# Sparse attention with two mixer layers: local scores as one 64x64 matmul per head

## The chip, the core and the metric

One core of a Trainium2 chip runs the whole program: TensorE (PE) multiplies, VectorE (DVE), ScalarE (ACT) and GpSimd (POOL) work on what it leaves, SyncE (SP) starts most of the DMAs. The metric is the time of one execution on the device in microseconds. The kernel before took 983.25 us (median of three runs, 981.56 to 983.28).

## The reference

Attention over four batches, eight heads, 576 tokens and 64 channels a head. Heads 0 to 3 are local (a query sees itself and the 31 tokens before it), heads 4 to 7 strided. Two mixer layers follow, each with a 512 to 2048 to 512 feed-forward part (FFN), which is most of the arithmetic.

```python
scores = 1 / np.sqrt(D) * np.matmul(q, k.transpose(0, 1, 3, 2))
rel = pos[:, None] - pos[None, :]
mask_local = (rel >= 0) & (rel < 32)
mask_strided = (rel >= 0) & (pos[None, :] % 32 == pos[:, None] % 32)
...
attn = softmax(np.where(masks, scores, -1e9))     # heads 0..3 local, 4..7 strided
x = np.matmul(attn, v)                            # then (B, S, 512)
...
u = x + (x.T @ U @ V).T                           # mixer 1: over tokens
y = u + np.maximum(u @ w_ch1, 0.0) @ w_ch2        # FFN of layer 1
...
u = y + np.real(np.fft.fft2(y))                   # mixer 2
out = u + np.maximum(norm(u) @ w21, 0.0) @ w22    # FFN of layer 2
```

## The kernel before, in words

**Stages.** Attention of batch 0, its token mix and the first weights come first (the startup). Then a main stream of FFN chunks runs on PE: lines 797 to 799 are the first FFN matmuls, lines 823 to 825 the second, in f16 pairs. Between them a fixed table (`TICKS`, then `RATES`) gives steps to two side streams: one makes FFN weights (raw 64-bit words are loaded, made into f32 by ACT and DVE, lines 133 to 137, then split), the other runs the attention of batches 1 to 3, the layout of FFN inputs and the Fourier part. The tile scheduler puts the instructions of all streams into one order for each engine by its own priorities and estimates; within an engine they then run in that order.

**Local attention.** A pair j of local heads (0 and 1, or 2 and 3) stands in SBUF with one head's 64 channels on partitions 0 to 63 and the other's on 64 to 127: k as 640 columns (tokens), q as columns of queries. A unit, `local_unit(b, j, u)`, scores four windows of 64 queries against 96 keys each (one window of u = 1 has 128). Line 386 writes the masks of all four windows into a PSUM bank (bf16 identity times mask), line 390 adds one f32 matmul a window on top. So that one matmul gives both heads, the queries were laid out with zeros: 128 columns a window, the first 64 with head 0's queries on the upper 64 partitions and zeros below, the others the reverse. Row 0 to 63 of the result is then head 0, row 64 to 127 head 1. Each batch has four units, so 16 such matmuls, 64 in all. Softmax follows (lines 357 to 365: DVE takes the maximum, ACT the exponential), then transposes on PE (line 398), an ACT copy (line 400), the product with v (line 406: weights of 64 columns, on the left or right half of the array) and the division.

**The rest.** Line 456 scores the 32 tokens left over of each half, with weights of 64 columns and all 128 partitions, left and right half of the array in turn, both into one bank. Line 472 takes their product with v on tiles of 64 rows by 32 columns: the upper rows (j = 0) into one bank, the lower (j = 1) into another. Line 422 is the strided scores.

**Loads.** `qk_load` (lines 301 to 314) brings k and q of a pair with two DMAs from SP's queue. Two local pairs stand early in the startup's list of loads (`LOADS`); each later pair takes a buffer that comes free, and batch 1's wait (line 296) until the first token mix is done.

Of the kernel before, what the change touches and what calls it, by code (L numbers as in the profile page):

```python
# [25 lines left out]
SG = 11  # L26
# [24 lines left out]


class Lane:
    """A stream of steps; a step that yields a name waits until that name is in flags."""

    def __init__(self, gen, flags):
        self.gen, self.flags = gen, flags
# [12 lines left out]
def fused_kernel(ctx: ExitStack, tc: tile.TileContext, ql, kl, vl, vr, qs, ks, vs, uraw, vraw,  # L70
                 w11, w12, w21, w22, cb, cf, ft, out):
    nc = tc.nc
    V, A, T, G, S = nc.vector, nc.scalar, nc.tensor, nc.gpsimd, nc.sync
# [15 lines left out]
    def bank():  # L89
        if wnow[0]:  # L90
            nbk[0] += 1
            z = BSEQ[nbk[0] % len(BSEQ)]
            if z:
                return (pf1, pf2)[z - 1].tile([128, 512], F32, tag=f"f{z}", name="bk")
        return pb.tile([128, 512], F32, tag="b", name="bk")
# [16 lines left out]
    flags = set()  # L112
# [133 lines left out]
    def p_buf():  # L246
        if wnow[0]:
            return early_buf("gh", 416)
        return atp.tile([128, 416], F32, tag="P", bufs=PB, name="P")

    def pt_buf():
        if wnow[0]:
            return early_buf("gl", 512)
        return atp.tile([128, 512], F32, tag="PT", bufs=PTB, name="PT")
# [39 lines left out]
    def gate(b, ap):  # L294
        if b == 1:
            A.activation(out=ap, in_=late[0], func=AF.Copy)
# [4 lines left out]
    def qk_load():  # L301
        b, x, j = QK[len(qk)]
        if len(qk) == 3:
            z = ub[3].rearrange("p a n -> p (a n)")
            q, k = z[:, 0:108 * SG], z[:, 108 * SG:108 * SG + 640]
        else:
            q = cst.tile([128, 108 * SG], F32, tag="q", bufs=3, name="q")
            k = cst.tile([128, 640], F32, tag="k", bufs=3, name="k")
            gate(b, q[0:1, 0:1])
            gate(b, k[0:1, 0:1])  # L310
        nq, nk = (1152, 640) if x == "l" else (108 * SG, 54 * SG)
        S.dma_start(out=k[:, 0:nk], in_=(kl if x == "l" else ks)[b, j])
        S.dma_start(out=q[:, 0:nq], in_=(ql if x == "l" else qs)[b, j])
        qk.append((q, k))

    def qk_upto(n):
        while len(qk) < min(n, len(QK)):
            qk_load()
# [23 lines left out]
    def first_loads():  # L342
        for x in LOADS:
            if x == "w":
                pre.append(wload(w11, len(pre), S))
            elif x == "m":
                mix_raw()
            elif x[0] in "ls":
                qk_load()
            else:  # L350
                loaded[x] = VT[x[0]](0, int(x[1:] or 0))

    def softmax_rows(P, Sb, r, groups):
        mx = atp.tile([128, 8], F32, tag="mx", bufs=3, name="mx")
        c = 0
        for o, n, w in groups:
            V.tensor_reduce(out=mx[r, c:c + n], in_=Sb[r, o:o + n * w].rearrange("p (n w) -> p n w", n=n),
                            axis=AX.X, op=ALU.max)
            c += n
        V.tensor_scalar(out=mx[r, 0:c], in0=mx[r, 0:c], scalar1=-0.125, scalar2=None, op0=ALU.mult)  # L360
        c = 0
        for o, n, w in groups:
            for i in range(n):
                a = o + i * w
                A.activation(out=P[r, a:a + w], in_=Sb[r, a:a + w], func=AF.Exp,  # L365
                             scale=0.125, bias=mx[r, c:c + 1])
                c += 1
# [5 lines left out]
    def norm_out(O, dst, r, n):  # L373
        Ov = O[r, 0:130 * n].rearrange("p (n h w) -> p n h w", h=2, w=65)
        rc = atp.tile([128, 3, 2, 1], F32, tag="rc", bufs=3, name="rc")
        recip(rc[r, 0:n], Ov[:, :, :, 64:65])
        V.tensor_tensor(out=dst.rearrange("p n (h w) -> p n h w", h=2), in0=Ov[:, :, :, 0:64],
                        in1=rc[r, 0:n].to_broadcast([r.stop - r.start, n, 2, 64]), op=ALU.mult)
# [4 lines left out]
    def local_unit(b, j, u, q, k, v):  # L383
        Sb = bank()
        n = LCOLS[u]
        T.matmul(Sb[:, 0:n], lhsT=idb, rhs=mL[u], start=True, stop=True)
        for g, x, o, w in LU[u]:
            w0 = LWIN[g, x][0]
            i = 128 * (2 * g + x)
            T.matmul(Sb[:, o:o + w], lhsT=q[:, i:i + 128], rhs=k[:, w0:w0 + w], start=False, stop=True,  # L390
                     skip_group_check=True)
        P = p_buf()
        softmax_rows(P, Sb, FULL, [(0, 3, 96), (288, 1, 128)] if u else [(0, 4, 96)])
        yield
        Tb = bank()
        m = 128 if u else 96
        for i, (g, x, o, w) in enumerate(LU[u]):
            T.transpose(Tb[0:m, 128 * i:128 * i + 128], P[:, o:o + m], ident)
        PT = pt_buf()
        A.activation(out=PT[0:m], in_=Tb[0:m], func=AF.Copy)  # L400
        yield
        O = bank()
        for i, (g, x, o, w) in enumerate(LU[u]):
            for h in range(2):
                c = 65 * (2 * (g % 2) + h)
                T.matmul(O[64 * x:64 * x + 64, c:c + 65],
                         lhsT=PT[0:w, 128 * i + 64 * h:128 * i + 64 * h + 64],
                         rhs=v[0:w, h, 2 * g + x, :], start=True, stop=True, skip_group_check=True)
        norm_out(O, ub[b][:, 2 * u:2 * u + 2, 128 * j:128 * j + 128], FULL, 2)
        yield  # L410
# [39 lines left out]
    def rest_unit(b, qks, v):  # L450
        p0 = 32 * b
        Sb = bank()
        T.matmul(Sb[:, 0:128], lhsT=idb, rhs=mX, start=True, stop=True)
        for j, (q, k) in enumerate(qks):
            for f in range(2):
                T.matmul(Sb[64 * f:64 * f + 64, 64 * j:64 * j + 64], lhsT=q[:, 1024 + 64 * f:1088 + 64 * f],
                         rhs=k[:, RWIN[f]:RWIN[f] + 64], start=False, stop=True, skip_group_check=True)
        P = p_buf()
        softmax_rows(P, Sb, FULL, [(0, 2, 64)])
        yield  # L460
        Tb = bank()
        T.transpose(Tb[:, 0:128], P[:, 0:128], ident)
        PT = pt_buf()
        A.activation(out=PT[:, 0:128], in_=Tb[:, 0:128], func=AF.Copy)
        yield
        r = slice(p0, p0 + 32)
        for j in range(2):
            O = bank()
            for f in range(2):
                for h in range(2):  # L470
                    c = 65 * (2 * f + h)
                    T.matmul(O[r, c:c + 65], lhsT=PT[64 * j:64 * j + 64, 64 * f + 32 * h:64 * f + 32 * h + 32],
                             rhs=v[64 * j:64 * j + 64, f, h, :], start=True, stop=True,
                             skip_group_check=True, tile_position=(64 * j, p0))
            norm_out(O, ur[r, :, 128 * j:128 * j + 128], r, 2)
        yield
# [461 lines left out]
    q = [0]  # L938
# [20 lines left out]
def _layout(np, q, k, v, mU, mV, w11, w12, w21, w22):  # L959
    import ml_dtypes  # L960
    pos, tiles, groups = _tok()
    f32 = np.float32
    B = q.shape[0]
# [3 lines left out]
    def put(dst, src, toks):  # L967
        i = [c for c, t in enumerate(toks) if t >= 0]
        dst[..., i] = src[:, [toks[c] for c in i]].transpose(0, 2, 1)

    def putv(dst, src, toks):
        i = [c for c, t in enumerate(toks) if t >= 0]
        dst[:, i, 0:64] = src[:, [toks[c] for c in i]]
        dst[:, i, 64] = 1.0

    ql = np.zeros((B, 2, 128, 1152), f32)
    kl = np.zeros((B, 2, 128, 640), f32)
    vl = np.zeros((B, 2, 128, 2, 8, 65), f32)
    vr = np.zeros((B, 128, 2, 2, 65), f32)
# [3 lines left out]
    for j in range(2):  # L983
        for hh in range(2):
            r = slice(64 * hh, 64 * hh + 64)
            h = 2 * j + hh
            put(kl[:, j, r], k[:, h], kext)
            for i in range(8):
                o = 128 * i + 64 * hh
                put(ql[:, j, r, o:o + 64], q[:, h], wins[i])  # L990
                w0, w = LWIN[i // 2, i % 2]
                putv(vl[:, j, :, hh, i], v[:, h], kext[w0:w0 + w])
            for f in range(2):
                o = 1024 + 64 * f + 32 * hh
                put(ql[:, j, r, o:o + 32], q[:, h], tiles[4 + f])
                putv(vr[:, 64 * j:64 * j + 64, f, hh], v[:, h], kext[RWIN[f]:RWIN[f] + 64])
            h += 4
            for i, toks in enumerate(groups):
                put(qs[:, j, r, 108 * i + 54 * hh:108 * i + 54 * hh + 54], q[:, h], toks)
                put(ks[:, j, r, 54 * i:54 * i + 54], k[:, h], toks)  # L1000
                t, e = divmod(i + (i > 0), 2)
                putv(vs[:, j, 64 * e:64 * e + 64, t, hh], v[:, h], toks)
    neg = -1e30
    mL = []
    for u in range(2):
        m = np.full((128, LCOLS[u]), neg, f32)
        for g, x, o, w in LU[u]:
            w0 = LWIN[g, x][0]
# [102 lines left out]
```

## Time and profile before

| what | value |
|---|---|
| median of three runs | 983.25 us (981.56 to 983.28) |
| span of the profiled execution | 979.2 us |
| what lies around the span, against the median | 4.05 us |
| PE busy | 935.3 us, 96% |
| weight loads of PE (PEld) busy | 522.8 us, 53% |
| DVE, ACT, POOL busy | 531.8, 360.4, 60.3 us |
| DMA | 76.53 MB, 78 GB/s mean |

The span is from the first instruction to the last; the time of an execution holds a little more. The profile gives no device time of its own for this execution, so what lies around its span is taken against the median. PE is the engine that is nearly always at work. Its matmuls are pipelined: a row's own duration is from its start to the modelled end of its last result, so how long one keeps the next from starting is read from the starts, not from the durations. f32 matmuls appear as two weight loads and two matmuls each.

### The profile page before, as it was taken

How to read it: one execution, taken by the hardware profiler on the slowest of the kernel's cores; microseconds unless marked ns; L12 is line 12 of the kernel's file. 1: busy time of each engine (PE TensorE's matmuls, PEld its weight loads, DVE VectorE, ACT ScalarE, POOL GpSimd, SP SyncE). 2: the span in 40 equal slices, each digit the busy share in tenths (PEclk: the TensorE clock that was granted, in tenths of full speed). 3: DMA queues.
4: the chain of work that ended last, by engine and by line, in shares of the span. 5: the costliest groups of instructions: out<-in, count | busy, mean ns of one | idle time of the engine just before them, and what ended most of it. 6: DMA issues, size and time to landing. Idle time of an engine off the chain costs nothing. (4 is left out here: it accounts for less than half of the span.)

```text
span 979.2 us, 13687 instructions
## 1 busy us (share of the span) xinstructions
PE 935.3 (96%) x5264; PEld 522.8 (53%) x5264; DVE 531.8 (54%) x1346; ACT 360.4 (37%) x885; POOL 60.3 (6%) x88
## 2 busy tenths in 40 slices
PE   4958999999999999999999989999999999999998
PEld 3746765556545564466445545544554444444465
DVE  4578798833342336853979998884235212122222
ACT  4667677624131334531546554231122101111011
POOL 0010111000000000100110400001001000100000
PEclk9558999999999999999999999999999999999999
DMA  9357666332201103602332610011002100300200
GB/s 301 131 175 236 217 217 212 95 115 94 64 16 28 39 3 116 172 1 44 108 107 88 151 44 1 1 33 55 1 1 43 44 1 6 80 1 1 46 20 22
DMA packets 60464, 76.53 MB, mean 78 GB/s; under 512 B 38064, under 2 KB 43440, under 8 KB 60400
## 3 DMA queue, kind: packets, MB, share of 16 engines
q1 hardware_dynamic: 51376, 42.53, 15.2%
q0 software_dynamic: 9024, 33.14, 10.6%
q8 instruction: 41, 0.67, 0.3%
q14 instruction: 23, 0.19, 0.1%
HBM read 60.18 MB, written 7.08 MB: 69 GB/s over the span
## 5 line engine op out<-in xcount | busy, mean ns | idle before, releaser
L797 PE MATMUL f<-ut,wslot 128*128 128x512 f16 (+1 forms) x672 | 236.1, 351 | 5.9 <-DVE gl L804 5.2
L798 PE MATMUL f<-ut,wslot 128*128 128x512 f16 (+1 forms) x672 | 235.8, 351 | 1.1 <-DMA ut<-lo 1.1
L799 PE MATMUL f<-ut,wslot 128*128 128x512 f16 (+1 forms) x672 | 235.6, 351 | 0.0
L823 PE MATMUL f<-wslot,gh 128*128 128x512 f16 x576 | 218.1, 379 | 0.9 <-DVE ub L831 0.5
L824 PE MATMUL f<-wslot,gh 128*128 128x512 f16 x576 | 218.1, 379 | 0.1
L825 PE MATMUL f<-wslot,gl 128*128 128x512 f16 x576 | 218.1, 379 | 0.0
L803 ACT ACTIVATE gh<-f 128x512 f16<-128x512 f32 (+1 forms) x168 | 89.4, 533 | 305.6 <-PE f L799 305.2
L804 DVE SCALAR_TENSOR_TENSOR gl<-f,gh 128x512 f16<-128x512 f32 (+1 forms) x168 | 102.8, 612 | 146.3 <-ACT gh L803 145.6
L831 DVE SCALAR_TENSOR_TENSOR ub<-f,ivt,ub 128x512 f32<-128x512 f32 x64 | 47.9, 748 | 130.1 <-PE f L825 129.8
L798 PEld LDWEIGHTS <-wslot 128*128 128x128 f16 x672 | 66.3, 99 | 64.3 <-issue 10.6
L797 PEld LDWEIGHTS <-wslot 128*128 128x128 f16 x672 | 66.4, 99 | 59.9 <-issue 4.9
L799 PEld LDWEIGHTS <-wslot 128*128 128x128 f16 x672 | 66.2, 98 | 58.9 <-issue 1.1
L825 PEld LDWEIGHTS <-gl 128*128 128x128 f16 x576 | 56.5, 98 | 66.9 <-issue 0.3
L823 PEld LDWEIGHTS <-gh 128*128 128x128 f16 x576 | 57.0, 99 | 63.8 <-issue 1.2
L824 PEld LDWEIGHTS <-gh 128*128 128x128 f16 x576 | 56.7, 98 | 62.7 <-issue 1.5
L153 ACT ACTIVATE wslot<-wslot,wsc 128x512 f16<-128x512 f32 x64 | 46.0, 718 | 43.1 <-DVE wslot L156 20.2
L133 ACT ACTIVATE wslot<-raw 128x512 f32<-128x512 f32 x64 | 42.9, 676 | 27.9 <-DMA raw<-in_w 26.5
L160 POOL DMA_DIRECT2D raw<-in_w x61 | 33.3, 546 | 319.1 <-DVE wslot L137 62.7
L156 DVE SCALAR_TENSOR_TENSOR wslot<-wslot,wsc 128x512 f16<-128x512 f32 x64 | 48.6, 760 | 7.6 <-ACT wslot L153 7.3
L197 ACT ACTIVATE wslot<-wslot 128x512 bf16<-128x512 f32 x64 | 40.3, 630 | 20.3 <-DVE wslot L137 15.9
L365 ACT ACTIVATE P<-bk,mx 108x64 f32<-108x64 f32 (+2 forms) x126 | 31.2, 328 | 39.2 <-DVE mx L360 35.9
L137 DVE SCALAR_TENSOR_TENSOR wslot<-raw,wslot 128x512 int32<-128x512 int32 x64 | 44.4, 697 | 0.1
(222 smaller groups left out, 953.3 us busy)
## 6 DMA issues: line engine op xcount, KB each, us to landing
raw<-in_w POOLq DMA_DIRECT2D x61, 512.0 KB, 4.0
q<-in_ql SPq DMA_DIRECT2D x8, 576.0 KB
q<-in_qs SPq DMA_DIRECT2D x7, 594.0 KB
out<-ub SPq DMA_DIRECT2D x16, 256.0 KB
vl<-in_vl SPq DMA_DIRECT2D x8, 390.0 KB
vs<-in_vs SPq DMA_DIRECT2D x8, 390.0 KB
k<-in_kl SPq DMA_DIRECT2D x8, 320.0 KB
scr<-xs SPq DMA_DIRECT2D x8, 270.0 KB
```

The source lines that it names most:

```text
L137: V.scalar_tensor_tensor(out=d, in0=hi, scalar=-0x80000000, in1=d, op0=ALU.bitwise_and, op1=ALU.bitwise_or)
L153: A.activation(out=dst, in_=src, func=AF.Copy, scale=s)
L156: V.scalar_tensor_tensor(out=dst, in0=src, scalar=s, in1=hi, op0=ALU.mult, op1=ALU.subtract)
L797: T.matmul(ps[:, 0:n], lhsT=wh, rhs=uh[:, k, cols], start=(k == 0), stop=False)
L798: T.matmul(ps[:, 0:n], lhsT=wh, rhs=ul[:, k, cols], start=False, stop=False)
L799: T.matmul(ps[:, 0:n], lhsT=wl, rhs=uh[:, k, cols], start=False, stop=(k == 3))
L803: A.activation(out=gh[:, i, cols], in_=ps[:, 0:n], func=AF.Relu)
L804: V.scalar_tensor_tensor(out=gl[:, i, cols], in0=ps[:, 0:n], scalar=0.0, in1=gh[:, i, cols], op0=ALU.max, op1=ALU.subtract)
L823: T.matmul(ps, lhsT=ga, rhs=w[:, 0, :], start=(i == 0), stop=False)
L824: T.matmul(ps, lhsT=ga, rhs=w[:, 1, :], start=False, stop=False)
L825: T.matmul(ps, lhsT=gb, rhs=w[:, 0, :], start=False, stop=(i == HW - 1))
L831: V.scalar_tensor_tensor(out=utile(t), in0=ps, scalar=iv, in1=utile(t), op0=ALU.mult, op1=ALU.add)
```

## The change

The queries of a local pair are laid out without the zeros: 64 columns a window, head 0 on the upper partitions, head 1 on the lower. The array q of a pair goes from 1152 to 640 columns (the 128 of the rest tokens keep their form and move from column 1024 to 512). Line 390's matmul of 128 by 128 becomes two of 64 by 64, one for each head: the upper left quarter of the array for head 0, the lower right for head 1. Both write the same bank, on partitions 0 to 63 and 64 to 127. Masks, softmax and all that follows are the same. An emptied comment line keeps the numbers up to 390; the new matmul is line 391, and all lines behind it are one higher than before.

```diff
@@ qk_load
-        nq, nk = (1152, 640) if x == "l" else (108 * SG, 54 * SG)
+        nq, nk = (640, 640) if x == "l" else (108 * SG, 54 * SG)
@@ local_unit
             w0 = LWIN[g, x][0]
-            i = 128 * (2 * g + x)
-            T.matmul(Sb[:, o:o + w], lhsT=q[:, i:i + 128], rhs=k[:, w0:w0 + w], start=False, stop=True,
-                     skip_group_check=True)
+            i = 64 * (2 * g + x)
+            for r in (slice(0, 64), slice(64, 128)):
+                T.matmul(Sb[r, o:o + w], lhsT=q[r, i:i + 64], rhs=k[r, w0:w0 + w], start=False, stop=True,
+                         skip_group_check=True)
@@ rest_unit
-                T.matmul(Sb[64 * f:64 * f + 64, 64 * j:64 * j + 64], lhsT=q[:, 1024 + 64 * f:1088 + 64 * f],
+                T.matmul(Sb[64 * f:64 * f + 64, 64 * j:64 * j + 64], lhsT=q[:, 512 + 64 * f:576 + 64 * f],
@@ _layout
-    ql = np.zeros((B, 2, 128, 1152), f32)
+    ql = np.zeros((B, 2, 128, 640), f32)
...
-                o = 128 * i + 64 * hh
+                o = 64 * i
                 put(ql[:, j, r, o:o + 64], q[:, h], wins[i])
...
-                o = 1024 + 64 * f + 32 * hh
+                o = 512 + 64 * f + 32 * hh
```

The scheduler sees twice the matmuls and sets some orders anew. On PE, at batch 1's second local unit, before (line 398 are transposes of the unit ahead, line 386 the mask, line 390 the scores; `bk` is a PSUM bank):

```order
L398 MATMUL bk<-ident,P 96x128
L386 LDWEIGHTS cbt
L386 MATMUL bk<-cbt 128x384
L398 MATMUL bk<-ident,P 96x128
L390 MATMUL bk<-k,q 128x96
L398 MATMUL bk<-ident,P 96x128 x2
L390 MATMUL bk<-k,q 128x96 x3
```

The same place on PE with the change (line 399 are the transposes, line 391 the scores):

```order
L399 MATMUL bk<-ident,P 96x128
L386 LDWEIGHTS cbt
L386 MATMUL bk<-cbt 128x384
L399 MATMUL bk<-ident,P 96x128
L391 MATMUL bk<-k,q 64x96
L399 MATMUL bk<-ident,P 96x128 x2
L391 MATMUL bk<-k,q 64x96 x7
```

The first score matmul still stands alone between transposes, but it is now one head's quarter; its partner stands behind the transposes with the other six. Six of the twelve units of batches 1 to 3 are parted so, a seventh as five and three; five stand in one piece.

On PE, at batch 1's scores of the rest tokens, before (line 453 is their mask, line 456 the scores, lines 797 to 799 the FFN):

```order
L398 MATMUL bk<-ident,P 128x128
L453 LDWEIGHTS cbt
L453 MATMUL bk<-cbt 128x128
L456 MATMUL bk<-k,q 64x64 x4
L797 LDWEIGHTS wslot
L797 MATMUL f_1206<-ut_614,wslot 128x256
L398 MATMUL bk<-ident,P 128x128
```

The same place on PE with the change (line 454 the mask, line 457 the scores):

```order
L399 MATMUL bk<-ident,P 128x128
L454 LDWEIGHTS cbt
L454 MATMUL bk<-cbt 128x128
L457 MATMUL bk<-k,q 64x64
L399 MATMUL bk<-ident,P 128x128
L457 MATMUL bk<-k,q 64x64 x2
L399 MATMUL bk<-ident,P 128x128 x2
L457 MATMUL bk<-k,q 64x64
```

The four matmuls on halves of the array stood together and now stand as one, two and one, with full-array transposes between. In batches 2 and 3 they stay together.

## Rows read from the trace of the kernel before

**Rows 1.** The page's totals: engine, busy us, share of the span, instructions.
```profile
PE 935.3 (96%) x5264; PEld 522.8 (53%) x5264; DVE 531.8 (54%) x1346; ACT 360.4 (37%) x885; POOL 60.3 (6%) x88
```

**Rows 2.** Busy time by stretch of the span; columns in the first row.
```profile
core 0: us, PE busy (x) PEld busy (x) DVE busy (x) ACT busy (x) POOL busy (x), PEclk, DMA share, GB/s
0.00:20.00 20.00, 8.52 (x52) 6.76 (x53) 7.05 (x21) 7.34 (x20) 1.42 (x6) 1.00 0.91 277
...
84.00:120.00 36.00, 32.03 (x330) 26.53 (x329) 28.49 (x87) 25.60 (x76) 3.70 (x7) 1.00 0.65 210
120.00:176.00 56.00, 53.40 (x305) 30.57 (x303) 50.44 (x102) 42.77 (x102) 7.92 (x15) 1.00 0.62 201
176.00:200.00 24.00, 23.71 (x172) 14.08 (x171) 19.86 (x57) 15.59 (x38) 0.00 (x0) 1.00 0.29 66
200.00:340.00 140.00, 140.00 (x848) 76.60 (x848) 50.31 (x116) 42.07 (x108) 0.00 (x0) 1.00 0.21 62
```

**Rows 3.** PE's waits, 82 to 200 us: waiting for, us, times, longest.
```profile
PE bk L398 <- ACT P L365: 2.7, 3, 1.3
PE bk L522 <- ACT x L518: 1.3, 2, 0.8
```

**Rows 4.** Line 390's instructions: count, ns min/median/max, first and last start, form.
```profile
L390 PEld LDWEIGHTS bk<-k,q x128: 187/192/337, 9.6 to 325.1; 128*128 128x128 f32 x128
L390 PE MATMUL bk<-k,q x128: 246/275/497, 9.6 to 325.2; 128*128 128x96 f32 x112, 128*128 128x128 f32 x16
```

**Rows 5.** Timeline at batch 2's first unit: start, us together, what, count.
```profile
177.56 0.33 PE L386 MATMUL bk<-cbt 128*128 128x384 bf16 x1
...
177.72 1.03 PE L390 MATMUL bk<-k,q 128*128 128x96 f32 x8
...
178.59 0.38 PE L797 MATMUL f<-ut,wslot 128*128 128x512 f16 x1
```

**Rows 6.** Timeline of PE at 95: two passes between transposes.
```profile
95.10 0.36 PE L390 MATMUL bk<-k,q 128*128 128x96 f32 x2
```

**Rows 7.** Timeline of PE in the startup; in brackets its idle time before.
```profile
9.62 1.99 PE L390 MATMUL bk<-k,q 128*128 128x96 f32 x8 [4.81 <-DMA q<-in_ql]
...
18.67 2.02 PE L390 MATMUL bk<-k,q 128*128 128x96 f32 x16 [1.07 <-DMA q<-in_ql]
```

**Rows 8.** Line 456's instructions (weights of 64 columns).
```profile
L456 PEld LDWEIGHTS bk<-k,q x32: 132/138/231, 27.1 to 332.1; 128*64 128x64 f32 x32
L456 PE MATMUL bk<-k,q x32: 222/222/369, 27.1 to 332.1; 128*64 128x64 f32 x32
```

**Rows 9.** Line 472 (tiles of 64 rows): first four, all sixteen, durations.
```profile
112.62 0.41 PE L472 MATMUL bk<-vr,PT 64*32 64x65 f32 x4
...
112.62 0.90 PE L472 MATMUL bk<-vr,PT 64*32 64x65 f32 x16
...
L472 PE MATMUL bk<-vr,PT x48: 214/217/241, 112.6 to 340.0; 64*32 64x65 f32 x48
```

**Rows 10.** Timeline at batch 1's rest scores, line 456, between full-array matmuls.
```profile
108.50 0.22 PE L453 MATMUL bk<-cbt 128*128 128x128 bf16 x1
...
108.65 0.31 PEld L456 LDWEIGHTS bk<-k,q 128*64 128x64 f32 x8 [0.16 <-issue]
108.65 0.45 PE L456 MATMUL bk<-k,q 128*64 128x64 f32 x8
...
109.03 0.28 PE L797 MATMUL f<-ut,wslot 128*128 128x256 f16 x1
```

**Rows 11.** Timeline of ACT in batch 1's attention.
```profile
93.45 0.66 ACT L133 ACTIVATE wslot<-raw 128x512 f32<-128x512 f32 x1 [1.42 <-DMA raw<-in_w]
```

**Rows 12.** The page's DMA issues: what, queue, count, size.
```profile
q<-in_ql SPq DMA_DIRECT2D x8, 576.0 KB
```

**Rows 13.** Timeline of PE ahead of the first FFN matmul.
```profile
74.96 1.22 PE L592 MATMUL bk<-idh,gh 128*128 128x128 f16 x8 [8.27 <-ACT gh L153]
```

## The prediction

> **What bounds the kernel now.** I read the page's totals first: TensorE (PE) is busy for 96% of the span [rows 1]. A mean over stages says little, so next the busy time by stretch [rows 2]: from 200 to 340 us PE is busy for all of the 140 us, from 176 to 200 for 23.71 of 24. There every microsecond that PE saves or loses is in the time. From 84 to 120 and from 120 to 176 it is busy for 32.03 of 36 and 53.40 of 56, so it waits for 6.6 us in all, mostly for results of ACT [rows 3]. Then the line that is changed [rows 4]: 128 weight loads and 128 matmuls, so each of the 64 local score matmuls is two passes. Four units of four windows belong to each batch. Batch 0 runs before the first FFN (its first pass at 9.62), batch 1 around 95, batch 2 from 177, batch 3 to 325 [rows 4 to 7]. So batches 2 and 3 lie where PE never waits, batch 1 where it waits a little, batch 0 in the start, which waits for loads.
>
> **The unit before.** At the full level of the clock (2.4 GHz, granted 1.00 [rows 2]) a unit's eight passes start at 177.72 and the next line starts at 178.59: 0.87 us, or 0.109 a pass [rows 5]. What sets this step? The pair at 95.10 lasts 0.36 together, so the second starts 0.36 - 0.275 = 0.085 behind the first [rows 4, 6]: with its weights already in place, 96 columns need 0.085. The steady 0.109 is then the load. A load of 128 columns takes 192 ns and one of 64 columns 138 [rows 4, 8]: 54 ns for 64 columns, so 0.108 for 128. The mask matmul stands 0.16 ahead of the first pass, which is its own stream of 384 columns: going over from it costs nothing [rows 5].
>
> **The unit after.** A quarter loads 64 columns (0.054) but streams the same 96 or 128 columns of keys: the halved contraction shortens nothing. So each pass takes 0.085, the stream is now the limit, and a 128-column window takes a third more. Do the two heads run side by side? In the rest unit's output line two row tiles at the same columns do: the first four passes, all on the upper rows, start (0.41 - 0.217)/3 = 0.064 apart, all sixteen (0.90 - 0.217)/15 = 0.046 apart [rows 9]. Column halves do too: the eight passes of line 456 last 0.45 together, less 0.22 for the last is 0.23 for seven steps, 0.033 each and so less than one load of 0.054 [rows 8, 10]. So I take the quarters as parallel: 8 x 0.085 = 0.68 a unit, a gain of 0.19.
>
> Those two rows leave one thing open: the row tiles of [rows 9] write to two PSUM banks, the column halves of [rows 10] to one bank but over all rows; no row shows two row tiles on one bank, which is what the change does. The Trainium skill speaks against it here: TensorEngine Tiling (Array Packing), section Restrictions and Gotchas, says that different row tiles cannot access the same bank simultaneously. By that rule the unit's passes would take turns, 0.68 more a unit; by the rows they don't. No trace here shows it, and it is a rival below.
>
> **What a visit to a small tile costs.** Line 453 (full array) starts at 108.50, line 456 on halves at 108.65, the next full-array matmul at 109.03 [rows 10]: 0.53. Off this go line 453's own 128 columns (0.05, a third of the 0.16 of [rows 5]) and four loads a half (4 x 0.054 = 0.22): about 0.25 remains for emptying the array twice and for the first load, which nothing covers (the loader stands idle for 0.16 there). A unit in one piece is then 0.68 + 0.25 = 0.93 against 0.87; with the 128-column window 0.1 more than before. Mean over the two: +0.075, for 12 units +0.9.
>
> The order adds more. In batches 1 to 3 the scheduler makes 19 visits of these 12 units: six units are parted 1 + 7 by full-array transposes and one 5 + 3. Before, a parting cost nothing. Now each adds 0.25, and 0.17 in which only one of the two quarters works (two passes): 0.42 x 7 = 2.9. Four are in batch 1, two in batch 2, one in batch 3. Batch 1's rest scores also go from one visit to three: 2 x 0.25 and one more pair, 0.6. By batch: 1: 0.3 + 1.7 + 0.6 = 2.6. 2: 0.3 + 0.8 = 1.15. 3: 0.3 + 0.4 = 0.7.
>
> Batches 2 and 3 are on the path: +1.9 (bounds 0.5, if a parting's extra visit were free, and 2.5). Batch 1: 2.6 against 6.6 of waits in the 92 us behind 84. Where PE waits for a weight or a softmax that hangs on DMA (ACT stands 1.42 for a raw weight at 93.45 [rows 11]), it may come later without harm; where ACT waits for PE's scores, the delay goes round. Bounds 0 and 2.6; I take 1.0, a little under half, since the waits are more than twice the delay. DVE and ACT get no other work, and their reads of the scores are the same.
>
> **The loads.** Each q load shrinks from 576 KB [rows 12] to 320 KB. 262,000 bytes at the 277 GB/s of the first 20 us [rows 2] are 0.95 us. PE stands 4.81 for the first q and 1.07 for the second [rows 7], whose SP queue holds both: first unit 0.9 earlier, second up to 1.9. But the bounds of what reaches the FFN are 0 and 1.9: between lie softmax, strided attention and the 8.27 for which PE waits ahead of the first transposes [rows 13], a chain over the scratch's DMAs that is moved whole only if all in it moves. I take 1.1, nearest to the 1.07 of the second wait. The six later q loads are not waited for by PE; 0, and what they free for raw weights is in batch 1's half.
>
> **Sum.** -1.1 + 1.0 + 1.9 = +1.8 us. The profiled execution's span is 979.2 and the median of the runs 983.25, so 4.05 lie around it; 979.2 + 1.8 + 4.05 = 985.1 us, 0.18% above the median. What a measurement of this kernel can tell from no change is about 0.2%, 1.97 us: the forecast is a change of nothing to slightly slower.
>
> **Rivals.**
> - Slower, with no cover: batch 1's visits hold up ACT's softmax, which holds up PE again, and the start's chain ends when it did. Its place is 84 to 176; for it speaks that ACT waits for PE's scores there, against it the 6.6 us of waits. -0 + 2.6 + 1.9 = +4.5: 987.8. It decides once less than 1 us of the 2.6 is hidden and the first FFN matmul comes less than 0.5 earlier.
> - The quarters take turns at the bank: 12 units x 0.68 = 8.2 on top of the forecast: 993.3. For it, no row of two row tiles on one bank; against it, column halves on one bank that run together [rows 10]. This is the skill's rule above.
> - Faster by the loads: all of 1.9 reaches the FFN, and batch 0's units, of which the first takes 1.99 where a later one takes 1.03 [rows 5, 7] (steps of 0.22, as at the half level, 1.2 GHz), give 0.3 too; batch 1's visits vanish in the waits. -2.2 + 0 + 1.9 = -0.3: 982.9. For it, the saturated start; against it, the 8.27.
> - The change does what its words suggest, and a quarter's pass costs half: if a pair took 0.058 (load-bound), 12 x 8 x 0.027 = 2.6 less than forecast: 982.5. Against it, the 0.085 with weights in place.
>
> **Chances.** Forecast 0.50, no cover 0.17, turns at the bank 0.06, loads 0.20, half cost 0.07. The forecast's own range is 983 to 987.2 and is cut by the +0.2% bound (985.2) about in the middle: 0.26 the same, 0.24 slower. Slower: 0.24 + 0.17 + 0.06, less 0.02 of no cover that ends lower: 0.45. Faster (under 981.3): a quarter of the loads' case and most of a half of the last, 0.05 + 0.03, and 0.02 from the forecast's edge: 0.10. The rest, 0.45, is the same. The range 981.3 to 988.8 leaves out the turns at the bank and the edges of the others, some 0.17.
>
> **What would show it.** Right: in a unit of one piece a pair of passes every 0.085, some 0.25 around it, and the next full-array line 0.93 behind the mask's end; lone quarters between transposes at 0.42 a visit; weight loads at 138 ns; in 200 to 340 still no wait of PE, and batch 2's stretch about 1 us longer; the second q wait gone, the first FFN matmul about 1 us earlier. Wrong: pairs at 0.17 (the bank), pairs at 0.058, visits that cost far from 0.25, or a first FFN matmul that moves by over 2 us either way.

## The result: slower by 0.9%, outside the range

Timed beside each other, 20 executions of each, the changed kernel took 989.25 us (median; 982.67 to 996.64), the kernel before 981.12 (972.69 to 988.21). The ratio is 1.0086, 95% interval 1.0056 to 1.0115: slower by 8.1 us of medians. The forecast was 985.1, 0.2% above the 983.25 it started from; its range ended at 988.8. (Medians are over all executions of a kernel; a ratio leaves out the ones over 1.5% above that kernel's fastest, so the two can differ by up to 0.7%.) The profiled execution took 996.64 us, the longest of the twenty, with a span of 994.8.

The page's totals of the changed kernel, as [rows 1]:

```profile
PE 947.5 (95%) x5392; PEld 521.8 (52%) x5392; DVE 531.4 (53%) x1346; ACT 361.3 (36%) x885; POOL 60.3 (6%) x88
```

DVE and ACT have the same work as before to within 1 us. The stretches of [rows 2] after the change (same columns):

```profile
0.00:20.00 20.00, 9.89 (x88) 6.98 (x88) 8.06 (x24) 7.99 (x21) 1.42 (x6) 1.00 0.92 281
84.00:120.00 36.00, 33.65 (x347) 25.12 (x345) 28.45 (x84) 25.03 (x71) 4.41 (x8) 1.00 0.62 198
120.00:176.00 56.00, 50.76 (x274) 28.55 (x274) 43.72 (x90) 38.20 (x91) 6.67 (x12) 0.94 0.56 177
176.00:200.00 24.00, 19.53 (x118) 9.34 (x116) 17.52 (x48) 13.82 (x32) 1.05 (x2) 0.93 0.40 88
200.00:340.00 140.00, 140.00 (x879) 74.91 (x876) 52.87 (x119) 42.47 (x107) 0.00 (x0) 1.00 0.18 52
```

From 200 us on PE still never waits. But from 120 to 200 it is busy for 70.29 of 80 us, where it was 77.11, DVE and ACT are *less* busy in these 80 us, not more, and the granted clock is no longer 1.00. Something else is late. PE's waits from 82 to 215 us name it (columns as in [rows 3]):

```profile
PE f L825 <- DVE wslot L156: 4.1, 3, 2.9
PE bk L523 <- ACT x L519: 1.8, 3, 0.9
...
PE f L824 <- ACT wslot L153: 1.3, 2, 0.8
PE bk L399 <- ACT P L365: 0.9, 1, 0.9
```

PE stands 5.4 us ahead of the second FFN product (lines 824, 825) for a weight that ACT and DVE have not split yet. Before, in the same 82 to 215 us, this wait was 0.4 in all:

```profile
PE f L823 <- ACT wslot L153: 0.4, 2, 0.2
```

Neither ACT nor DVE has a new instruction.

The score matmul itself did what the prediction said. Its rows as [rows 4], then the unit as [rows 5], a lone quarter (two passes) between transposes as [rows 6], and the rest scores in three visits as [rows 10]:

```profile
L391 PEld LDWEIGHTS bk<-k,q x256: 128/133/228, 8.0 to 337.0; 64*64 64x64 f32 x128
L391 PE MATMUL bk<-k,q x256: 240/243/419, 8.0 to 337.1; 64*64 64x96 f32 x115, 64*64 64x128 f32 x13
```

```profile
91.86 0.27 PE L399 MATMUL bk<-ident,P 128*96 128x128 f32 x1
92.06 0.38 PE L391 MATMUL bk<-k,q 64*64 64x96 f32 x2
92.37 0.42 PE L399 MATMUL bk<-ident,P 128*96 128x128 f32 x2
...
105.16 0.33 PE L457 MATMUL bk<-k,q 128*64 128x64 f32 x2
105.42 0.33 PE L399 MATMUL bk<-ident,P 128*128 128x128 f32 x1
105.67 0.34 PE L457 MATMUL bk<-k,q 128*64 128x64 f32 x4
...
106.31 0.33 PE L457 MATMUL bk<-k,q 128*64 128x64 f32 x2
...
183.29 0.33 PE L386 MATMUL bk<-cbt 128*128 128x384 bf16 x1
183.55 0.88 PE L391 MATMUL bk<-k,q 64*64 64x96 f32 x16
184.36 0.39 PE L798 MATMUL f<-ut,wslot 128*128 128x512 f16 x1
```

Sixteen passes last 0.88 together, the last of them 0.243: 0.64 for fifteen steps, 0.085 for the two heads' pair. From mask to next FFN line the unit takes 1.07 where it took 1.03. The two quarters run side by side on one bank. By the Trainium skill's rule for row tiles (TensorEngine Tiling (Array Packing), section Restrictions and Gotchas) they would take turns, and this trace does not agree.

So I looked for the loss between two marks that PE's stream reaches in every kernel: the first eviction of the first FFN product on DVE, and the eighth eviction of the second. Here they are for before, then after (start, us, engine, line):

```profile
81.37 0.42 DVE L804 SCALAR_TENSOR_TENSOR gl<-f,gh 128x256 f16<-128x256 f32 x1 [0.96 <-ACT gh L803]
...
213.75 0.75 DVE L831 SCALAR_TENSOR_TENSOR ub<-f,ivt,ub 128x512 f32<-128x512 f32 x1 [1.54 <-PE f L825]
```

```profile
78.85 0.42 DVE L805 SCALAR_TENSOR_TENSOR gl<-f,gh 128x256 f16<-128x256 f32 x1 [1.76 <-ACT gh L804]
...
225.29 0.75 DVE L832 SCALAR_TENSOR_TENSOR ub<-f,ivt,ub 128x512 f32<-128x512 f32 x1 [1.54 <-PE f L826]
```

132.4 us before, 146.4 after. I call this the *stretch*; it holds batches 1 and 2, and no part of the start. A stretch is read from one profiled execution of each kernel. Kernels with the same matmuls in the same order differ in it by 0.5 (132.4 before, 131.9 in experiment 1) and by 3.0 (146.4 after, 143.4 in experiment 2, 143.8 in experiment 12), so a single difference of that size shows nothing. By these the change costs 11 to 14 us of the stretch, more than the 8.1 of the medians; why the medians differ by less was not found.

### The profile page after: what moved, and what is told of

Its sections match the earlier page's. It is cut to its first block, busy times and chain, and to the rows that moved or that the text cites. A ratio compares the mean times of both kernels' runs of the same rounds, so it can differ in the third digit from the quotient of the medians.

```text
span 994.8 us, 13945 instructions
## 1 busy us (share of the span) xinstructions
PE 947.5 (95%) x5392; PEld 521.8 (52%) x5392; DVE 531.4 (53%) x1346; ACT 361.3 (36%) x885; POOL 60.3 (6%) x88
## 5 line engine op out<-in xcount | busy, mean ns | idle before, releaser
L825 PE MATMUL f<-wslot,gh 128*128 128x512 f16 x576 | 219.0, 380 | 4.1 <-DVE wslot L156 4.1
L824 PE MATMUL f<-wslot,gh 128*128 128x512 f16 x576 | 218.3, 381 | 3.0 <-DVE ub L832 1.7
L825 PEld LDWEIGHTS <-gh 128*128 128x128 f16 x576 | 56.6, 98 | 65.6 <-issue 3.9
L824 PEld LDWEIGHTS <-gh 128*128 128x128 f16 x576 | 57.2, 99 | 64.4 <-issue 1.8
L153 ACT ACTIVATE wslot<-wslot,wsc 128x512 f16<-128x512 f32 x64 | 46.0, 718 | 55.0 <-DVE wslot L156 28.2
L156 DVE SCALAR_TENSOR_TENSOR wslot<-wslot,wsc 128x512 f16<-128x512 f32 x64 | 48.6, 759 | 6.4 <-ACT wslot L153 6.2
L365 ACT ACTIVATE P<-bk,mx 108x64 f32<-108x64 f32 (+2 forms) x126 | 30.6, 329 | 37.7 <-DVE mx L360 33.8
```

What stands on the lines that cost most here:

```text
L153: A.activation(out=dst, in_=src, func=AF.Copy, scale=s)
L156: V.scalar_tensor_tensor(out=dst, in0=src, scalar=s, in1=hi, op0=ALU.mult, op1=ALU.subtract)
L824: T.matmul(ps, lhsT=ga, rhs=w[:, 0, :], start=(i == 0), stop=False)
L825: T.matmul(ps, lhsT=ga, rhs=w[:, 1, :], start=False, stop=False)
```

## The experiments

Before any of them ran, the orders could be compared. With the small loads alone every engine keeps the order of before. With the quarters, even with the old large loads, PE, DVE and ACT get the changed kernel's order. So it is the matmuls and not the loads that move the scheduler. On DVE and ACT the two orders part at 88 us of the changed kernel and are the same again behind 206. So the change has three parts that can be taken apart: the loads, the quarters, and the order. Theory O blames the order, theory Q the quarters (visits to the small tile), theory L the loads.

To hold an order, a kernel got a table of instruction numbers for each engine and, for each neighbouring pair in it, an edge on the same engine that asks for order only, no wait (long lines are cut at `...`):

```diff
+ORD = {
...
+    "DVE":
+        "0 8 1 9 2+2 5 19 6 4 7 18 22 20+2 23+2 12+3 ...
...
+    for e, runs in ORD.items():
...
+                    tc.add_manual_dep(y, prev.name, mybir.DependencyInfo(mybir.DependencyClass.NoSync, ...
```

Kernels with a table have line numbers some 81 higher: L906 there is L825 here, L905 L824, L480 L399, L446 L365, L237 L156, L234 L153, L215 L134.

**1. The loads alone.**

```diff
-            for r in (slice(0, 64), slice(64, 128)):
-                T.matmul(Sb[r, o:o + w], lhsT=q[r, i:i + 64], rhs=k[r, w0:w0 + w], ...
+            T.matmul(Sb[:, o:o + w], lhsT=q[:, i:i + 128], rhs=k[:, w0:w0 + w], ...
```

> The small q loads alone: q has 640 columns as in the changed kernel, the scores are again one 128x128 matmul per window, which reads 128 of these columns (so the second head's scores are of other queries than the reference's; amount of work and shapes are those of before). Every engine has the order of the kernel before. Theory O (the loss is the new order of the instructions on DVE, ACT and PE): about 978, since the first FFN matmul came 3.3 us earlier in the changed kernel and nothing is paid for it. Theory Q (the loss is the quarters themselves: visits to the small tile, lone quarters): the same, 978. Theory L (the loss comes from the loads, which land at other times and collide with weight loads later): 985 or more.

Measured: 981.37 us; before 983.97 in the same comparison; ratio 1.0017 (0.9971 to 1.0063). Stretch 131.9. Nothing is lost by the loads: theory L falls. No gain can be told either.

**2. The quarters alone**, with the old loads: in place of `q[r, i:i + 64]` the weights are `q[r, i + r.start:i + r.stop]` with `i = 128 * (2 * g + x)`.

> The quarters alone: q with its zero blocks and 576 KB as before, eight 64x64 matmuls a unit. All engines have the order of the changed kernel. Theory O and theory Q: about 992, the changed kernel's 989 plus the 3.3 us that the small loads gave at the start. Theory L: about 983, before plus my own 1.9 for the switches.

Measured: 989.74 (before, as above, 983.97), ratio 1.0125 (1.0048 to 1.0203), stretch 143.4. The loss comes with the eight matmuls.

**3. Everything, in the order of before** (table from the kernel before, each score matmul replaced by its two quarters).

> The whole change, quarters and small loads, but PE, DVE and ACT are held to the order of the kernel before (each score matmul replaced by its two quarters in place). Theory O: 979 to 982: minus 3.3 for the start, plus 1 to 3 for the switches. Theory Q: as the changed kernel, 988 to 990, since the same quarters are there. Theory L: also 988 to 990.

Measured: 979.79, ratio 1.0014 (0.9975 to 1.0053), stretch 135.6. Same quarters and loads as the changed kernel, 20 visits of the units of batches 1 to 3 instead of 19, and in the times the loss is gone. Theory Q falls for all but a small part: the stretch is 3.6 longer than in experiment 1.

**4. The reverse**: the matmuls of experiment 1, held to the changed kernel's order.

> The reverse: the 128x128 score matmuls of before with the small q loads (the second head's scores are of other queries than the reference's), but PE, DVE and ACT are held to the order of the changed kernel. Theory O: slow as the changed kernel, 986 to 990, though no matmul is on a small tile. Theory Q: as with the loads alone, about 978. Theory L: 988 to 990.

Measured: 991.28, ratio 1.0105 (1.0038 to 1.0173), stretch 140.0. Without the quarters it is as slow as the changed kernel, with PE's waits for weights (here L904 is line 823 of before; columns as in [rows 3]):

```profile
PE f L905 <- DVE wslot L237: 2.6, 2, 1.5
PE f L904 <- ACT wslot L234: 2.0, 2, 1.5
```

Theory O holds, from both sides. The four kernels make a square of stretches: whole matmuls in the old order 131.9, quarters in the old order 135.6, whole matmuls in the new order 140.0, quarters in the new order 143.4 to 146.4. The new order adds 8.1 without the quarters and 7.8 to 10.8 with them.

**5. Whose order?** PE in the order of before, DVE and ACT in the changed one.

> The whole change with a mixed order: PE is held to the order of the kernel before, DVE and ACT to the order of the changed kernel. Theory D (the loss is the order on DVE and ACT: the weights of the second FFN product are made too late, PE waits for them): slow, 988 to 991, with PE's waits for a weight ahead of the second FFN product at about 115 to 120 and about 187 still there. Theory P (the loss is where the score units and transposes stand on PE, and DVE and ACT only follow): as with the whole order kept, 979 to 982, without these waits.

Measured: 989.53, before 981.48 in the same comparison, ratio 1.0083 (1.0043 to 1.0123), stretch 144.0. Theory D as to the engines: DVE and ACT. (The reverse, PE alone in the new order, was not run.) The waits were not the ones I expected: over the stretch PE waits 2.0 us for weights of the second product and 5.1 for exponentials, and near 187 it is an exponential. PE there, then ACT (start, us, engine, line; in brackets the idle time before):

```profile
183.19 0.38 PE L881 MATMUL f<-ut,wslot 128*128 128x512 f16 x1
186.51 0.31 PE L480 MATMUL bk<-ident,P 128*96 128x128 f32 x1 [2.95 <-ACT P L446]
```

```profile
183.19 0.72 ACT L234 ACTIVATE wslot<-wslot,wsc 128x512 f16<-128x512 f32 x1 [2.01 <-DVE sct L224]
183.82 1.32 ACT L234 ACTIVATE hi<-ub,sct 128x512 f16<-128x512 f32 x2
185.04 0.58 ACT L885 ACTIVATE gh<-f 128x512 f16<-128x512 f32 x1
185.52 0.71 ACT L234 ACTIVATE wslot<-wslot,wsc 128x512 f16<-128x512 f32 x1
186.13 0.79 ACT L446 ACTIVATE P<-bk,mx 128x96 f32<-128x96 f32 x3
```

The same place in experiment 3, where the first exponential stands ahead of the weight:

```profile
171.69 0.34 ACT L446 ACTIVATE P<-bk,mx 128x96 f32<-128x96 f32 x1 [2.16 <-DVE mx L441]
171.93 0.71 ACT L234 ACTIVATE wslot<-wslot,wsc 128x512 f16<-128x512 f32 x1
172.54 0.71 ACT L234 ACTIVATE hi<-ub,sct 128x512 f16<-128x512 f32 x1
```

This is what an order is worth on an engine that runs it strictly: ACT has nothing more to do, but five instructions stand ahead of the exponentials, the first of them stands 2.01 us for a scale of DVE's, and PE stands 2.95 for the lot.

**6. A version that might beat both**: as 3, but the seven parted units are put together on PE, which saves eight visits.

> The whole change in the order of before on DVE and ACT, and on PE too, but for the seven score units that this order parts: their eight quarters stand together, where the last of them stood, so eight visits to the small tile fall away. By my 0.25 a visit: 2.0 less than with the parted units, about 978, and PE's lag against the loads-alone kernel between the first FFN line and 215 us falls from 3.5 to about 1.5. Rival: a visit costs nothing and the 3.5 are waits; then it stays at 980 and the lag at 3.5.

Measured: 977.31 beside 981.48, ratio 0.9985 (0.9946 to 1.0025), stretch 134.5. The lag behind experiment 1 over the stretch falls from 3.6 to 2.5. Seven of the eight visits lie in the stretch (the eighth is batch 3's), so this would be 0.16 a visit, where I had used 0.25. But 1.1 is a difference of two single executions, and kernels of the same order differ by 0.5: the price is not settled by it. The time is not told apart from that of the kernel before.

**7. A third order**: the two steps that split a weight get the precedence of the FFN's evictions.

```diff
+            with tc.high_priority(HP):
                 split_hi(sls[i][:, 0, :], w, sc)
                 split_lo(sls[i][:, 1, :], w, sc, sls[i][:, 0, :])
```

> The changed kernel in a third order: the two steps that split a finished weight (ACT's high half, DVE's low half) are given the precedence that the FFN's own evictions have, all else is left to the scheduler. If the loss is the late weights alone (theory D in its simple form), PE's waits for them go, some 4 to 5 us, and the time is about 984. Rival: every other order moves the wait elsewhere; then 988 or more.

Measured: 992.03, ratio 1.0117 (1.0058 to 1.0175), stretch 140.1. PE still waits 3.8 us for weights, so the step that was to take these waits away did not, and the simple form of theory D is not tested by it (experiment 5, with 2.0 us of such waits, speaks against it). Precedence for the last link of a weight's chain did not bring the weight forward; which link holds it there I did not test.

**8 and 9. Where in the stretch?** PE in the order of before; DVE and ACT switch order at about 135 us.

> The whole change, PE in the order of before; DVE and ACT in the changed kernel's order up to the end of the first stretch (some 135 us: DVE's 258th, ACT's 225th instruction, where both orders have issued the same set), from there in the order of before. Theory A (the losses of the stretches add up): of the lag that the mixed order gathered against the kept order, 2.3 us came before that point and 6.1 behind it, so this one is about 982. Theory C (the later waits only follow from the early delay): slow, 988 or more.

> The reverse: DVE and ACT in the order of before up to that point, from there to 205 us in the changed kernel's order; behind that the orders are the same anyway. PE in the order of before. Theory A: about 986, and DVE's waits for raw weights (some 5 to 6 us, four times) and PE's wait of 3 us near 187 are there. Theory C: as with the kept order, 980.

Measured, beside 984.64 for the kernel before: early part 983.05, ratio 1.0027 (0.9982 to 1.0072), stretch 138.0; late part 987.31, ratio 1.0061 (1.0023 to 1.0099), stretch 141.8. Against the 135.6 of experiment 3 that is 2.4 and 6.2, together 8.6; both in one (experiment 5) 8.4. As far as single executions can tell, the losses add up and most of it lies behind 135 us; in the times, the late part alone is told apart from the kernel before, the early part is not.

**10. DVE's order alone.**

> The whole change, PE and ACT in the order of before, DVE alone in the changed kernel's order all through. If DVE's order carries the loss (its steps stand behind raw weights that have not landed, and ACT and PE wait for DVE): 986 to 990. If ACT's order does, or only both together: 979 to 983.

Measured: 984.12 beside the same 984.64, ratio 1.0024 (0.9988 to 1.006), stretch 142.1. In the profiled execution DVE alone brings 6.6 of the 8.4, with SP's queue, which no table holds, in the order of before. The timed runs lie between the two expectations and are not told apart from the kernel before, so how the loss divides between DVE and ACT stays open.

One sign goes with the order through all these runs: DVE's waits from 85 to 215 us for raw weights that have not landed. In experiment 5 and then in 3 (waiting for, us, times, longest):

```profile
DVE raw L215 <- DMA raw<-in_w: 5.9, 4, 3.3
```

```profile
DVE raw L215 <- DMA raw<-in_w: 1.5, 2, 1.0
```

It is 4.5 to 6.8 in all kernels whose DVE has the changed order in the late part, 0.5 to 1.5 in those with the order of before there (experiment 7, a third order: 3.0). Whether these waits cause PE's or only go with them was not tested.

**11 and 12. One wait taken away, and a control.** The longest single wait of the changed kernel can be read to its end. DVE and SP in it (same columns):

```profile
194.12 0.75 DVE L156 SCALAR_TENSOR_TENSOR lo<-ub,sct,hi 128x512 f16<-128x512 f32 x1 [3.67 <-DMA ut<-lo]
194.79 0.74 DVE L156 SCALAR_TENSOR_TENSOR wslot<-wslot,wsc 128x512 f16<-128x512 f32 x1
```

```profile
187.31 2.62 SPq L601 DMA_TRANSPOSE ut<-hi  x2
190.03 3.49 SPq L601 DMA_TRANSPOSE ut<-lo  x2
```

And PE, behind the transposes of 192.44:

```profile
195.59 0.38 PE L825 MATMUL f<-wslot,gh 128*128 128x512 f16 x1 [2.87 <-DVE wslot L156]
```

`lo` has two buffers. The transposes that read them now stand behind both `hi`; DVE, writing the third `lo`, stands 3.67 for a buffer, the split of a weight stands behind it, and PE stands 2.87 for that weight. Before, they went hi, lo, hi, lo, and DVE waited 0.8. The transposes follow DVE's and ACT's order. Experiment 11 holds the order of all three engines and sets only these eight transposes back; 12 holds and changes nothing.

```diff
-                S.dma_start_transpose(out=UT[key][i][:, :, 128 * j:128 * j + 128], in_=x)
+                t = S.dma_start_transpose(out=UT[key][i][:, :, 128 * j:128 * j + 128], in_=x)
+                if last and key == (0, 1):
+                    tc.add_manual_dep(t.ins, last[0].name, ...
+                last[:] = [t.ins]
```

> The changed kernel, PE, DVE and ACT held to its own order, and on SP's queue alone one thing changed: the eight DMA transposes of the second chunk's inputs go hi, lo, hi, lo as in the kernel before, in place of hi, hi, lo, lo. Theory T (near 190 DVE stands for the lo buffer that these transposes read, with the split of a weight behind it for which PE waits): DVE's wait of 3.7 us falls to about 1, PE's wait of 2.9 ahead of the second FFN product's line at about 190 goes to 0.5 or less, and the stretch from the first FFN eviction to the eighth eviction of the second product is 2 to 4 us shorter than with the order held alone. Rival: the weight is late for another reason, and the wait stays over 2 us.

> Control: the changed kernel with PE, DVE and ACT held to its own order, so nothing is changed. It should take what the changed kernel takes, 988 to 990; if holding an order cost or gave something by itself, it would differ by that. The stretch between the two evictions should be 143 to 147, DVE's waits for raw weights 5 to 7 us.

Measured: 988.11, ratio 1.0102 (1.0027 to 1.0178), stretch 142.1, against the control's 988.55, 1.0072 (1.0028 to 1.0116), 143.8. The kernel before took 987.08 in this comparison, more than in the others, so the control is judged by its ratio, 1.0072 beside the changed kernel's 1.0086, and by its stretch, 143.8 beside 146.4 and 143.4: within these intervals holding an order costs nothing by itself. PE's waits, 70 to 215 us, in 11 (here L911 is line 825), then 12:

```profile
PE bk L480 <- ACT P L446: 2.8, 2, 2.2
...
PE f L911 <- DVE wslot L237: 1.4, 2, 1.0
```

```profile
PE f L906 <- DVE wslot L237: 4.1, 3, 2.7
...
PE bk L480 <- ACT P L446: 1.0, 1, 1.0
```

PE's wait of 2.7 for the weight went as theory T says, and DVE's for the buffer fell from 3.5 to 0.8. But DVE now stands 1.9 for ACT's `hi` ahead of the next `lo`, and a wait of PE for exponentials, 2.2 at 181.24, took most of the place of the other. The stretch is 1.7 shorter, less than the 2 to 4 expected; one dip of the clock in the control (granted 0.77 and 0.89 in 110 to 120) would also give that, and the times are the same. One wait mended is not the order mended.

## Why the prediction was wrong

- **The step that failed** is one sentence: "DVE and ACT get no other work, and their reads of the scores are the same." True, and beside the point. I had compared the orders on PE, found the partings, priced them, and taken DVE, ACT and SP's queue as unchanged because their instructions are. The sum put this term at nothing, for no reason but that. Their *order* changed over 115 us, and this is most of the loss: ratio 1.0083 with DVE and ACT's new order against 1.0014 with the old, with PE the same; 8.4 us of the stretch, where the whole change costs 11 to 14. The rivals lacked it too: "no cover" had batch 1's stretch as the place, with ACT waiting for PE. In the trace it begins at the other end: PE waits for ACT and DVE, whose new order has them stand for raw weights, buffers and scales.
- **Batches 1 to 3, 1.0 for the first and 1.9 for the others: right in kind, a little small.** With the order held, the lag behind experiment 1 grows by 3.6 over the stretch (batches 1 and 2; forecast 1.0 + 1.15) and by 0.3 more at batch 3 (0.7): 3.9 against 2.9. The 3.6 is nearer to the 3.75 of the rival in which none of batch 1's 2.6 is hidden (2.6 + 1.15) than to the 2.15 I took, but it is one execution each; how much was hidden is not shown. Pairs every 0.085 and the unit 0.04 longer than before (forecast 0.06) are as said. A lone quarter between transposes takes 0.51 (91.86 to 92.37) less the step of the transpose itself, which is 0.11 to 0.15 in these traces: 0.36 to 0.40 against 0.42. The price of a visit around a whole unit is near the 0.25 said: 1.07 less 0.16 for the mask's stream [rows 5] and 0.68 for the passes leaves 0.23. The 0.16 for a visit saved in experiment 6 is less, and less sure.
- **The loads, -1.1: not shown.** In the profile after, as [rows 7] and [rows 13], the second q wait is gone and the transposes ahead of the FFN come 3.3 earlier:

```profile
8.03 1.55 PE L391 MATMUL bk<-k,q 64*64 64x96 f32 x16 [3.23 <-DMA q<-in_ql]
...
17.16 2.93 PE L391 MATMUL bk<-k,q 64*64 64x96 f32 x32
...
71.64 1.22 PE L593 MATMUL bk<-idh,gh 128*128 128x128 f16 x8 [5.57 <-ACT gh L153]
```

  But the first eviction came at 81.4 and 78.9, 79.6 with large and small loads, and at 71.0 and 72.1, 71.0 in other executions, again large and small: the start takes one of two courses, 9.5 us apart in the mean, with either size of loads (last section). Experiment 1's ratio is 1.0017. With 0 for the loads my own terms make +2.9, which the 0.9975 to 1.0053 of experiment 3 allows and doesn't prove.
- **The bank and the half cost: rightly put low.** The unit's 0.81 from the first pass to the next line excludes both (by the bank it would be some 1.5, with a pair at half cost 0.6).
- "In 200 to 340 still no wait" came true. I had named "visits that cost far from 0.25" and the bank as what would prove me wrong, and nothing about who waits between 120 and 200. A third sign, a first FFN matmul that moves by over 2 us, was there (first eviction 81.4 before, 78.9 after), but with a start that moves by more than that by itself it says nothing. And the 0.2% that I took a measurement to tell from nothing was too fine: with 20 executions of each the interval reaches 0.3% to either side.

## What to carry to other kernels

Where a scheduler sets the order, a change that doubles some instructions of one engine can re-order the others too: compare the order on every engine and queue, and where it differs, price a wait on an in-order engine and all that stands behind it. To learn whether an operation or its new order is to blame, hold the old order with edges that ask for nothing but order: here it separated in two runs what the reading of one trace had not. A row of a profile that moved by some microseconds is no effect until a second execution has it at the same place.

## What the runs showed of the hardware

**Two courses of the start.** Between 24 and 52 us the same strided matmuls last 375 ns in some executions and 252 in others. In all five profiled executions with 375 the first eviction comes at 77.4 to 83.9, in all nine with 252 at 69.0 to 72.5. Rows of before, after, and experiment 1 (line, engine, names, shapes, count, busy us, mean ns):

```profile
L422 PE MATMUL bk<-ub 128*108 128x54 f32 x22 | 4.3, 375 | 0.0
```

```profile
L423 PE MATMUL bk<-ub 128*108 128x54 f32 x22 | 4.3, 375 | 0.0
```

```profile
L422 PE MATMUL bk<-ub 128*108 128x54 f32 x22 | 2.4, 252 | 0.0
```

In before the granted clock of 25 to 40 us is 0.50, the 1.2 GHz level; in experiment 1 it is 1.00 up to 35. In after it reads 1.00 from 25 to 50, and the matmuls are as slow as in before: durations tell the pace there, the column does not. (The passes at 9.62 in [rows 7] are likewise some 0.21 apart, twice the 0.109 of [rows 5], where [rows 2] has 1.00.) Why an execution takes one course stays open; it moves the first eviction by 9.5 us in the mean, as much as the effect studied here. Behind the stretch executions differ as much: from the eighth eviction to the end 765.4 us in before, 775.9 in experiment 2, in kernels of either order (765.4 to 773.3 with the old one, 766.7 to 775.9 with the new).

**A wait of PE can cost twice.** The changed kernel's stretches around 120, 155 and 195 us, two of them here (columns as in [rows 2]):

```profile
120.00:125.00 5.00, 4.38 (x22) 2.96 (x22) 3.90 (x8) 3.05 (x5) 0.58 (x1) 0.66 0.31 98
...
195.00:200.00 5.00, 4.41 (x26) 2.05 (x26) 3.39 (x9) 2.84 (x7) 0.00 (x0) 0.66 0.49 99
```

Each follows waits of PE (0.79 and 1.01 ahead of 119.03 and 120.42, 0.92 and 0.88 ahead of 153.00 and 154.27, 2.87 ahead of 195.59). The matmuls bear the column out here: an FFN pass that keeps the next line waiting for 0.22 at 117.65 keeps it for 0.43 at 122.40. A mean of 0.66 over 5 us is 1.7 us of full speed lost, on top of the wait. Over the whole stretch the column has 0.97 in the changed kernel and 0.99 in experiment 2, whose order is the same: 3 us by this sum, the size of the difference between their stretches (146.4 and 143.4). In experiment 5 waits of the same kind, 2.95 at 186.51 among them, had no such fall between 100 and 205 us, so it doesn't always come.
